# Packed attention with a convolution gate: whole float32 words in batch 0's first layer, and group 4's keys and queries loaded as whole rows

## The chip, the cores and the metric

The kernel runs on one NeuronCore of a Trainium2 chip. It uses five engines with queues of their own: PE (matrix multiplies, with PEld for the loading of the stationary operand), DVE (vector work), ACT (activations and copies), POOL (set-up only here) and SP, which issues the transfers; transfers run on 16 DMA engines. The metric is the device time of one execution in microseconds (us), as a median over runs.

## What is computed

Batch 8, 8 heads, 576 positions, 64 numbers per head; p holds 32 packed queries per head. q, k, v and p come as float32, the three weights as float64.

```python
def sm_attn(qq, kk, vv):
    s = scale * np.matmul(qq, kk.transpose(0, 1, 3, 2))
    s = s - np.max(s, axis=-1, keepdims=True)
    a = np.exp(s)
    a = a / (np.sum(a, axis=-1, keepdims=True) + 1e-09)
    return np.matmul(a, vv)
p_packed = sm_attn(p, k, v)
out = sm_attn(q, p_packed, p_packed)
...
h = np.maximum(x @ w_in, 0.0)           # x: [B, S, 512], w_in: [512, 1024]
conv_out = sum(conv_w[k] * hp[:, k:k + S, :] for k in range(3))
gate = 1.0 / (1.0 + np.exp(-conv_out))
return (h * gate @ w_out).astype(np.float32)
```

So there are two attentions (the packed queries read the sequence, then the sequence reads the 32 packed rows), a first layer with relu, a gate from a convolution over three positions, and a second layer.

## The kernel before

**Tiling.** Four heads make a group; a batch has two groups, so there are 16 groups (group g belongs to batch g // 2). A group's attention (`attention`, L489) runs: first scores on PE (L450), their maximum on DVE (L495), exp on ACT (L499), the transposed weights (on PE at L525 with a copy at L528, from group 10 on by DVE and 16 transfers), the product with the values (L535), scaling and a transpose (L546, L551, L554), second scores (L450), then the second softmax on DVE and ACT (L559 to L578) and a transpose back (L583). The softmax's result is kept as two fp32r parts: `a2hi` (ACT, L587) and the remainder `a2lo` (DVE, L589).

The packed rows are multiplied with `w_in` beforehand: `packed_weight(b, hf)` (L599) gives, for each half hf of the 1024 columns, a weight `gw` for the batch, again as two parts: `ghi` by a copy on ACT (L621), and `glo`, for batches 0 and 1 by subtracting `ghi` in PSUM with PE (L625) and a second copy on ACT (L629), later with DVE (L632). `ffn1(b, j)` (L640) is the first layer, one of eight blocks of 128 columns: twelve fp32r multiplies of 288 columns (two groups, two halves of the sequence, and the products hi·hi, lo·hi, hi·lo) at L661; relu (L673), the three taps (L677, L679, L683), tanh (L687) and the gate (L689). `ffn2(m)` (L710) is the second layer for 128 rows of the output, with 24 multiplies of 512 columns (L752), a copy (L760) and the store (L762).

**Weights.** Eight tiles: 0 to 3 are parts of `w_in` (the first half of the columns needs 0 and 1, the second 2 and 3), 4 to 7 of `w_out`. Each is loaded (`load_weight`, 1024 KB) and made from float64 into float32 by ACT (L265) and DVE (L267, L272); those of `w_out` are split further by ACT, PE (L328) and ACT.

**Keys and queries** come in two ways (`by_block`, L356). For groups 0 to 3 a tensor is one transfer of whole rows (576 KB, 128 pieces of 4608 B), transposed on PE in nine 128 x 128 transposes, five and then four (L434), each set copied by ACT (L440). From group 4 on it is four transfers of 144 KB with pieces of 128 B (L405) and one DVE transpose (L417).

**Order.** `ORDER` (L21) is a text of two-digit numbers in base 36, each naming a stream (a load, a group's attention, a step of a layer); at each mention the stream's next step is issued. Every engine and SP works its queue in this order. `Flow` (L64) is a plan of times beside it: it reckons when each step would start, and before the second layer starts it puts multiplies of the identity into PE's queue wherever PE would wait (`fill`, L133; `warm`, L241, L244). Transfer times in the plan are multiplied by the factors in `SLOW` (L84).

**Buffers.** Accumulation tiles `big` in PSUM have three buffers, shared by scores, PE transposes, `packed_weight`, the weight split and the first layer; `h` has three, `gw` two, `a2` four, and `kq` three for the loads of groups 2 and up.

The order before, by queue, at its beginning (T5 and T4 are the two sets of PE transposes, s1 and s2 the scores, pv the product with the values, pk `packed_weight`, f1 b.j `ffn1`):

- SP: k0, q0, p(0), k1, w2, v0, conv_w, k2, w0, q1, v1, w1, k3, p(1), q2, v2, w5, w3, k4, w4, q3, v3, w6, k5, w7, v4, ...
- PE: kT0 T5, kT0 T4, qT0 T5, s1(0), kT1, ..., pk(0,0), pv(2), s1(3), minus(0,0), s2(2), f1 0.0, f1 0.1, f1 0.2, pk(0,1), ...
- DVE, from group 0's second softmax on: L559(0), maximum, w0 first half, subtract, w0 second half, sum, multiply, maximum of group 2, L583(0), w1 first half, L559(1), maximum, subtract, w1 second half, sum, a2lo(0), multiply, L583(1), ..., a2lo(1), ...

Of the kernel before, what the change touches and what calls it, by code (L numbers as in the profile page):

```python
# [18 lines left out]


ORDER = (  # L21
    "0002043m0408043u0304030305060b3l0c06013k050b060c0g0c0c0b060605053q3v3k0e06070e070a3k063v06063k0j060e3v09060j3s0k"
    "0f0j0o060k0e0f3n0k0i0h3r3r060k0d063k0e0m0d3k3r060d0r0e0e0d060e060e060m060e0m0r3t0m0m3t0s0r400e3w0w0s0e0s0n0z0e0e"
    "3t0s0l0e0n060z0z0l0l0e3y170e46460m0q060m0e0u0e0u0l0m460m0e41460p410m170m0e0m0u17480u3x493x480v410v0m0u3x48410m4a"
    "49484a10474849474a3z0m414948413z491f4a49124248470u0u4a4a474b124b0t490u124b0t14433z0u0t0m4a434b0m4c0t4d1f4b4b434c"
    "0u441f4d0x4c4b3z12120u4e18434e3z1a0u4c120m4d4c4g3o6e130u1a154c3z0u131a124c6e450m0u434e4d45126e0u4e434g4f0m456e4g"
    "1a0u1n0m0u124f6e1n451l4d4e4f6e0u454f4d1a4h1c4e4e0u0u4f4g1b0y1k4d451b4i4f4f114j4i7e1n7e4k4i6e1g4h6f4j6e6e4i6f6e4k"
    "4h4k4i4j4i7f161i121a4k4j4i6e1i6f6f121e1a4j4k4l7f1d126f6f6f6f4j4k4l1i6f1o4k6g121s4l1i4l6g4h124l7g4m1a4l6f1a1j4m1q"
    "191j1i1a6f4m4j121i6g1q7g1w6g6h6e4n6g4m6h1q204n1a1v6g1i6g4m1v4l1h6g4m1a4n124m121r1v4n6g6g236f7h1a6g4o121i4n1i4o4p"
    "6h6h4o4p4p1a236h124o7h4o6h4n1q6g4p1a6h6h6h4p6h4o1m4o1a1y4n234p4p1q1i6h1i1q4q282b1y4r6i1r1y6i1y1a1i6i126i6i1q1a2b"  # L30
    "4r6i12241a4q4q1z6i6j1a6i1a4r1i6i6i4s6i2b1p4s6j4s1q4t4u1q4s1i1y1i4t4s264t1t4t1q1z6k1y2g6j2c4u6j1y4u4s261i6j2j4u6j"
    "4s6k6j264u2j4v4t2j1q6j271i4u1u4v226i4u6j266j4t2e1x4w2k6j4t1i4v1q2e1i1q6k4w2e4v2a1i1q6h2f2e4v3p6k6k6k4w1y1i274x26"
    "6k1q6k6l1y4x6l216k6k6k2f4x1q6k4x2m1y4v50266m1q6l6l4w264v1q2r2m6l2h4w6l2m2r506l4x2r6l4y4w1q4y291y6l6l4w501q4y6l6m"
    "4z6m4z262o2n4x1q6m4z2e6m4y6m6m2z1y4x4z6m264y4y4z524z1y4y52524z6l6m251y522s6m34536n535354542e6m2m542e26512u526n6n"
    "6o6n546j6n261y516n532z54526n2z6n6n6n52541y376n516o376p5554553753536m6o262u6o2w552e5630266o6o55266o5635535655266o"
    "6o57552n5756551y56566o2i6p6o1y586p262u6p586q562e596p262d58596p6p6n596p2m6p1y586p6q58576p2m2e6o2u57595a1y5732592m"
    "6q2l1y58586q57266q596q6q3232572m3f2m6q362q6q592e266r6q5b6q262m6r3f2e265a5b6r6r6s6p6r6r5a5c2m6r6s2e5d6r6r5c2e6r5c"
    "5d2m5b5c5c5d5e6r2m6s2e5c6s5e325c5f2u2e5d5e5e6r5d5d383f5e5f2e6s5f5e336s6s6t2v5f6s6s2e6t5k3a2m5d2p2u6s5f5f6s5k5g6t"
    "5e2m3c5g3a2x6t5g2v6t5h2m6t2e6q2m6t2u6t6u2e325k2m6t6u5h2u6t5h6t5f5h5i5h6t3g5h2e5i6u2m5i6u2t2y6u6u5h6u5j333a3a6v5g"
    "6u5j2u6u6u5i5g5i5j326u6v2u3i5j2m5i5j5j5i6v6v6v2m5g5m2u6v6u5m5j5m2u5n6v2u5g325m6v3a6v6w5m6v3d5m3i6w5n5n6v5o5m6w6w"  # L40
    "32313i6w3b6x3i6w5n32325o3a5l5n5o6w3j5l6v5o6w6x32326w6w5o3b325n2u325p6w6x6y5n325l5p3j6x5q6s5o5o6x3a2u5r6x6x5p6x5p"
    "2u5q5q5r6x6x5r6y5p5p3a5q3i6x3e6z5r5p325s2u5q6x325q5s2u5r6y2u6y6y6y3a5q5s5t6z396y2u6y5r5r6y5t6y3a3i5u5t5s6y5t5s3a"
    "325s2u5t325t5s5u325v5t6z326z6z5u6z6w6z3i703i6z703i6z3a6z5v5w5w5v3a5x6z3a5y703a5w5x5w705y5w5w703h5y7070705y5w706y"
    "705x5x713a70715z5z3a5x5y3i64715y703i3i715x3i5x5y5z7172713a5z5z3i3a6071716071603a605z7161717264603i6z60613i723i3a"
    "3i5z726172727271617260727261627372627373626274636261733i73616473743i653i6263736573637363636273736673636674747466"
    "6367676667747474667466687574676872746675676967657568676969767569756a6969756976757575756b6a75776a686a76766a6b6b76"
    "6a7676767675766b76776a6c77786c77776b766b6b7768686c776d6d776c776d7777786c6d6c686d7878786c74786d787878786d79797a79"
    "79797979797a787979787b7a7a7a7a7977797b7a7a7a7a7c7a7b7b7b7b7a7b7b7c7b7b7b7c7c7d7c7c7d7c7c7c7c7d7d7d7d7d7d7d7b7c7d"
    "7d7d7d7d7d7d7i7d7d7c7d7i7d"
)  # L50


# [132 lines left out]
def tile_packed_attention_conv_gate(  # L185
# [303 lines left out]
    def attention(g):  # L489
        G = grp[g]  # L490
        yield Step("PE", 556, after=[("pT", g), ("kT", g)] + [("s1", g - 1)] * (g > 0), take=["big", "a1"], give=["kT", "pT"], sets=[("s1", g)], cols=1152, tiled=True)
        t = score(G["pT"], G["kT"], g)
# [90 lines left out]
        nc.vector.transpose(out=at, in_=s2)  # L583
# [56 lines left out]
    def ffn1(b, j):  # L640
# [15 lines left out]
        for gg in range(NG):
            ah, al = grp[NG * b + gg]["a2"]
            for w, xs in ((hi, (ah, al)), (lo, (ah,))):
                for x in xs:
                    for hf in range(2):  # L660
                        nc.tensor.matmul(  # L661
                            out=t[:, hf, :SH],
                            lhsT=w[:, gg, js],
                            rhs=x[:, hf * SH : (hf + 1) * SH],
                            start=n == 0,
                            stop=n == 3 * NG - 1,
                        )
# [153 lines left out]
```

## Time and profile before

| | us |
|---|---|
| median of 3 runs | 407.02 (406.36 to 407.58) |
| profiled execution | 406.22 |
| its span | 404.4 |
| PE busy | 395.5 (98% of the span) |
| DVE busy | 340.2 (84%) |
| ACT busy | 275.2 (68%) |

A span runs from the first to the last instruction of the profiled execution; the execution's own time is 1.8 us longer. Busy time is the union of an engine's instructions. In the rows below, a line of a group shows the source line, engine and operation, output and inputs with their shapes and count, then busy time and the mean of one in ns, then idle time just before it and what released it. A line of the order of time begins with start and length in us. The page gives the granted PE clock as full in every fortieth of the span, and the DMA engines as nearly full in the first fifth.

### The profile page before, as it was taken

The numbers are of one execution on the slowest core, as the hardware profiler recorded it, in microseconds if no ns is written. First come the engines' busy times: TensorE is split into PE (matmuls) and PEld (weight loads), VectorE is DVE, ScalarE is ACT, GpSimd is POOL, SyncE is SP. The second block draws the span as 40 slices with busy tenths as digits, with TensorE's granted clock in tenths as the row PEclk, the third lists the DMA queues.
The fourth block names the chain that finished last, engine by engine and source line by source line (L and its number), as shares of the span: only waits on it lengthen the run. The fifth ranks groups of instructions, "written<-read, shape, count | busy, mean of one in ns | idle before, by whom it ended". The sixth has DMA issues, their size and how long they took to land.

```text
span 404.4 us, 8231 instructions
## 1 busy us (share of the span) xinstructions
PE 395.5 (98%) x3319; PEld 317.6 (79%) x3319; DVE 340.2 (84%) x494; ACT 275.2 (68%) x475; POOL 0.9 (0%) x12
## 2 busy tenths in 40 slices
PE   7899999999999999999999999999999999999996
PEld 6668677787868878888778788788687878887886
DVE  0789999999999999999999999999889886557220
ACT  4889999977668486867566756687666676655121
POOL 0000000000000000000000000000000000000000
PEclk9999999999999999999999999999999999999999
DMA  8999999997947876496563715316001000010211
GB/s 298 366 366 233 293 257 163 137 157 128 134 96 105 129 190 128 88 186 103 107 99 99 151 55 101 129 30 113 28 2 52 28 18 35 26 53 0 78 53 52
DMA packets 140377, 49.19 MB, mean 122 GB/s; under 512 B 121244, under 2 KB 132788, under 8 KB 140340
## 3 DMA queue, kind: packets, MB, share of 16 engines
q1 hardware_dynamic: 140340, 48.67, 53.9%
q8 instruction: 26, 0.43, 0.5%
q14 instruction: 11, 0.09, 0.1%
HBM read 37.25 MB, written 9.44 MB: 115 GB/s over the span
## 4 chain that ended last, share of the span: by engine, by line
PE 74%; DMA 8%; ACT 8%; DVE 5%; SPq 3%; issue 1%; ACTq 0%
PE fo L752 42%; PE big L661 19%; PE sm L752 3%; DMA hgt<-in_moe_w_in_dram 3%; PE big L450 3%; PE big L609 2%; PE sm L535 2%; SPq L515 2%; DMA s<-in_moe_conv_w_dram 2%; DMA v<-in_v_dram 2%; ACT hgt L677 1%; ACT hbuf L673 1%; ACT hgt L687 1%; ACT wo_hi L323 1%; PE big L525 1%
## 5 line engine op out<-in xcount | busy, mean ns | idle before, releaser
L752 PE MATMUL fo<-wo_hi,xhi 128*128 128x512 f32 (+1 forms) x272 | 109.8, 404 | 0.7 <-ACT o L760 0.7
L752 PE MATMUL fo<-wo_hi,xlo 128*128 128x512 f32 (+1 forms) x272 | 106.5, 392 | 0.0
L752 PE MATMUL fo<-wo_lo,xhi 128*128 128x512 f32 (+1 forms) x272 | 106.1, 390 | 0.0
L673 ACT ACTIVATE hbuf<-big 128x576 f32<-128x576 f32 x64 | 41.8, 657 | 32.2 <-PE big L661 32.1
L752 PEld LDWEIGHTS fo<-wo_hi,xhi 128*128 128x128 f32 x272 | 51.2, 188 | 15.7 <-issue 3.0
L679 DVE SCALAR_TENSOR_TENSOR hgt<-hbuf,cw,hgt 128x576 f32<-128x576 f32 x64 | 51.2, 806 | 13.7 <-ACT hgt L677 13.3
L752 PEld LDWEIGHTS fo<-wo_hi,xlo 128*128 128x128 f32 x272 | 51.1, 188 | 12.3
L703 DVE TENSOR_TENSOR xlo<-hgt,xhi 128x1024 fp32r<-128x1024 f32 (+1 forms) x44 | 44.7, 1021 | 16.7 <-ACT xhi L700 16.6
L752 PEld LDWEIGHTS fo<-wo_lo,xhi 128*128 128x128 f32 x272 | 51.1, 188 | 8.5
L661 PE MATMUL big<-a2hi,ghi 128*128 128x288 f32 x256 | 55.8, 299 | 0.1
L687 ACT ACTIVATE hgt<-hgt 128x576 f32<-128x576 f32 x64 | 43.7, 690 | 15.9 <-DVE hgt L683 15.7
L661 PE MATMUL big<-a2hi,glo 128*128 128x288 f32 x256 | 54.4, 294 | 0.0
L661 PE MATMUL big<-a2lo,ghi 128*128 128x288 f32 x256 | 54.2, 293 | 0.0
L683 DVE SCALAR_TENSOR_TENSOR hgt<-hbuf,cw,hgt 128x576 f32<-128x576 f32 x64 | 50.8, 804 | 0.4
L689 DVE SCALAR_TENSOR_TENSOR hgt<-hgt,hbuf 128x576 f32<-128x576 f32 x64 | 47.2, 744 | 4.6 <-ACT hgt L687 4.3
L677 ACT ACTIVATE hgt<-hbuf,cw 128x576 f32<-128x576 f32 x64 | 49.8, 783 | 0.9
L661 PEld LDWEIGHTS big<-a2hi,ghi 128*128 128x128 f32 x256 | 42.9, 188 | 5.9 <-ACT glo L629 1.0
L700 ACT CAST xhi<-hgt 128x1024 fp32r<-128x1024 f32 (+1 forms) x44 | 38.9, 891 | 10.8 <-PE fo L752 6.4
L760 ACT COPY o<-fo 128x512 f32<-128x512 f32 (+1 forms) x34 | 19.6, 578 | 33.3 <-PE fo L752 28.7
L661 PEld LDWEIGHTS big<-a2lo,ghi 128*128 128x128 f32 x256 | 40.9, 188 | 0.0
L661 PEld LDWEIGHTS big<-a2hi,glo 128*128 128x128 f32 x256 | 40.8, 188 | 0.0
L495 DVE TENSOR_REDUCE nm<-big 128x1 f32<-128x576 f32 x16 | 11.9, 746 | 10.6 <-PE big L450 10.6
(91 smaller groups left out, 494.1 us busy)
## 6 DMA issues: line engine op xcount, KB each, us to landing
out_dram<-o SPq DMA_DIRECT2D x35, 256.0 KB, 2.5
v<-in_v_dram SPq DMA_DIRECT2D x16, 512.0 KB, 5.8
k<-in_k_dram SPq DMA_DIRECT2D x48, 144.0 KB, 4.1
q<-in_q_dram SPq DMA_DIRECT2D x48, 144.0 KB, 4.1
hgt<-in_moe_w_in_dram SPq DMA_DIRECT2D x3, 1024.0 KB, 11.2
hgt<-in_moe_w_out_dram SPq DMA_DIRECT2D x3, 1024.0 KB, 6.5
a1T<-stage SPq DMA_DIRECT2D x96, 20.0 KB, 1.8
hgt<-in_k_dram SPq DMA_DIRECT2D x2, 576.0 KB, 5.0
```

Source lines behind the costliest of these rows:

```text
L450: nc.tensor.matmul(out=o.rearrange("c (j r) -> c j r", r=NR) if by_block(g) else o, lhsT=lhs[r, 32 * i : 32 * i + 32], rhs=rhs[r, :, h, :] ...
L661: nc.tensor.matmul(out=t[:, hf, :SH], lhsT=w[:, gg, js], rhs=x[:, hf * SH : (hf + 1) * SH], start=n == 0, stop=n == 3 * NG - 1,)
L673: nc.scalar.activation(out=h[:, 1 : S + 1].rearrange("c (f s) -> c f s", f=2), in_=t[:, :, :SH], func=AF.Relu, scale=0.5)
L677: nc.scalar.activation(out=d, in_=h[:, 1 : S + 1], func=AF.Copy, scale=cw[:, NJ + j : NJ + j + 1])
L679: nc.vector.scalar_tensor_tensor(out=d, in0=h[:, 0:S], scalar=cw[:, j : j + 1], in1=d, op0=ALU.mult, op1=ALU.add)
L683: nc.vector.scalar_tensor_tensor(out=d, in0=h[:, 2 : S + 2], scalar=cw[:, 2 * NJ + j : 2 * NJ + j + 1], in1=d, op0=ALU.mult, op1=ALU.add)
L687: nc.scalar.activation(out=d, in_=d, func=AF.Tanh)
L689: nc.vector.scalar_tensor_tensor(out=d, in0=d, scalar=1.0, in1=h[:, 1 : S + 1], op0=ALU.add, op1=ALU.mult)
L700: nc.scalar.copy(out=hi[:, js, o], in_=src[:, js])
L703: nc.vector.tensor_tensor(out=lo[:, js, o], in0=src[:, js], in1=hi[:, js, o].bitcast(F32), op=ALU.subtract)
L752: nc.tensor.matmul(out=t[:, : fs.stop - fs.start], lhsT=x[:, c, :], rhs=w[:, c, fs], start=c + i == 0, stop=c == NJ - 1 and i == 2)
L760: nc.scalar.copy(out=o[:, fs], in_=sums_of[m, q][:, : fs.stop - fs.start])
```

## The change

Five things change.

1. `by_block` holds for group 4 too: its keys and queries are one 576 KB transfer each, transposed by PE (18 transposes and four copies on ACT) instead of eight transfers and two DVE transposes. The scores of group 4 read and write their blocks in the other order accordingly.
2. For batch 0 (`WHOLE = 1`) the second softmax's result of groups 0 and 1 stays one float32 tile (`a2whole`, straight from DVE's transpose), and `gw` one float32 tile (one copy on ACT): no `a2hi`, `a2lo`, no subtraction on PE, no second copy.
3. Batch 0's eight first-layer steps multiply whole float32 words: four multiplies of 288 columns in place of twelve in fp32r.
4. The plan's factors for transfer times change, and with them the number and places of the fillers.
5. `ORDER` is new throughout.

```diff
-    SLOW = ((4600, 1.28), (5500, 1.7))
+    SLOW = ((4600, 1.28), (5500, 1.15), (16500, 1.0), (56000, 1.085))
...
+    WHOLE = 1
...
-        return g < NG * 2
+        return g < NG * 2 + 1
...
+        if g < NG * WHOLE:
+            yield Step("DVE", 669, take=["a2"], give=["s2"], sets=[("hi", g), ("a2", g)])
+            at = wk.tile([128, S], F32, name="a2whole", tag="a2hi", bufs=4)
+            nc.vector.transpose(out=at, in_=s2)
+            G["a2"] = (at,)
+            return
...
+        if b < WHOLE:
+            yield Step("ACT", 904, give=["big"], sets=[("gw", b, hf)])
+            whole = wk.tile([128, NG, 512], F32, name="gwhole", tag="ghi")
+            nc.scalar.copy(out=whole, in_=t)
+            gw[b, hf] = (whole,)
+            return
...
-        yield Step("PE", 1563, after=after, take=["big", "h"], give=give, sets=[("f1", b, j)], cols=3456)
-        hi, lo = gw[b, j // 4]
+        whole = b < WHOLE
+        yield Step("PE", 1930 if whole else 1563, after=after, take=["big", "h"], give=give, sets=[("f1", b, j)], cols=4608 if whole else 3456)
+        parts = gw[b, j // 4]
...
+        last = (1 if whole else 3) * NG - 1
         for gg in range(NG):
-            ah, al = grp[NG * b + gg]["a2"]
-            for w, xs in ((hi, (ah, al)), (lo, (ah,))):
-                for x in xs:
+            xs = grp[NG * b + gg]["a2"]
+            for k, w in enumerate(parts):
+                for x in xs[: len(xs) - k]:
                     for hf in range(2):
                         nc.tensor.matmul(
...
-                            stop=n == 3 * NG - 1,
+                            stop=n == last,
```

The new order, by queue, at its beginning:

- SP: p(0), k0, p(1), conv_w, k2, q0, k1, v0, w1, q1, v1, w0, k3, q2, v2, k4, w2, w4, w3, q3, v3, w5, q4, k5, v4, w6, k6, w7, ...
- PE: kT0 T5, kT0 T4, s1(0), qT0 T5, kT1 T5, L525(0), qT0 T4, kT1 T4, pv(0), s1(1), ..., s2(1), ..., qT2 T5, pk(0,0), qT2 T4, pv(2), s1(3), kT4 T5, s2(2), f1 0.0, kT4 T4, f1 0.1, L525(3), f1 0.2, s1(4), qT3 T5, f1 0.3, the split of w4, pk(0,1), pv(3), qT3 T4, f1 0.4, f1 0.5, ...
- ACT, around the first step of the first layer: whole copy of gw(0,0), pb(2), qT2's second copy, ppT(2), queries of group 5, `minus`, kT4's first copy, exp of group 3, two of the queries, w2, relu of f1 0.0, ...
- DVE, from group 0's second softmax on: L559(0), maximum, subtract, w1 second half, sum, maximum of group 2, multiply, w0 first half, L559(1), w0 second half, maximum, subtract, whole transpose (0), sum, multiply, maximum of group 3, whole transpose (1), L559(2), ...

Runs of PE steps that use 64-row or 32-column tiles (s1, s2, pv, pk) without another step between number 29 in the old order and 26 in the new.

More of the change, by code (lines that the diff above doesn't have):

```diff
@@ L21 @@
 ORDER = (
[L22 to L46, printed above, removed]
@@ L47 @@
-    "6a7676767675766b76776a6c77786c77776b766b6b7768686c776d6d776c776d7777786c6d6c686d7878786c74786d787878786d79797a79"
-    "79797979797a787979787b7a7a7a7a7977797b7a7a7a7a7c7a7b7b7b7b7a7b7b7c7b7b7b7c7c7d7c7c7d7c7c7c7c7d7d7d7d7d7d7d7b7c7d"
-    "7d7d7d7d7d7d7i7d7d7c7d7i7d"
+    "3m030300043n3k0g030b0b0404040b020j06060508010c3k0j06060505070c060c3s0j06070a3k0c093k3q0e060o0605063k0e060e3t0k0i"
+    "0k0k3t060f060k0e0e0h3k060f060d3t0r060d0d0m0e0e0d0e0e060e060m060m0m3r0r0w0r0s3r0e0z3r0s0e0e0m0n0s0z0s0l0z060e0l46"
@@ new lines @@
+    "0l0m0n0u3u0e460m0m0l100m0m0e170e173l100e0u0e0u0m3y0m17480v1f3v103v3w4810490m0u483z493v0q4a0u3z480v49480p484a123z"
+    "0t491f3x0t3z484a3x40123x124b3z0y0m494a494b0m471f4b490u474a4a414b0m0t4c410t4a0m3z144d0u4c41120x0u4241414b4b4c1c0u"
+    "0m12440u183o4b4d4c0m416e1a4c1n4c1k134e4d430u6e0u4c4e110m1n6e4e430u110u436e431n134f4d4f1a4g1a0u121g4e4545431a0u0m"
+    "4g454g1b1243120u6e111a1b4d456e154f0u4e4d12110u454g4f4d120u121a4e451i1a1m0u4f4h1v1i4e1v4f4i4f1i4i4j7e1v4i1o4k7e12"
+    "4j6e4i4j121a6f6f4k6e6e6e4h4h7f166e121i1d4j6f4i196f4k1s6f4j1i1q1a4j124k121i1t1e1j4j1j7f234k1a1i4h6f231q6f4i1q4k12"
@@ new lines @@
+    "4i231a6g4l122b6f4m4m4k1a1w6f4l6f1q6g6e1i127g1i4n1l1h4m1q4l1y1a6f1q4m4n1y4l4l4n1i1y1r4q6g6g7g1a4l286g1r6h4n4m126g"
+    "4l4m6g1i4o6g6g1a4o6g201z4n1y244m214p1q4o1u4o4n6h6g7h4p2b1i4o6h6h2b1q4p1z7h1a6h4o6h6g4p1a4p4p6h6h6h6h4n1q4o4p124r"
+    "1y6i6h1a6i4q6h2j1a1y261i4q1a1a4r6i6i6i1p266i6i2c4s1i264s6i4r4s266i4s6f6j264t1i1q4s2e4t4t274s6i6j1i4u1q1y4t1y1i2o"
+    "6i4s6j2e6j4u6k6j1y6j4u2j1q1i4t4u2p1i4t2j4v6j2e6j276j4t4v6j6j1x3p6k4w4v1i6k2g4w502k26221y4w2e4v4w26504u6l1q2m4w4u"
+    "1y294v506k1q6k4w6k6k4u6l2r6k6j4v2w6k4v6k6k4x1y6l6m6l4x1i1q2r4x6l2r6m2z6l6l4y6k2f6l1q2m6i266l1q4w2m1q1y1q2e4y6l4y"
@@ new lines @@
+    "4x4y1y4x251q264y6l2f1q4x4z4x6m4z6m6m4z6m2m4z4y6m2z6m2z522q2s522e4z26374y4z2u512652514z6n532h2n6m535252532a6n266m"
+    "54526m6n536n52536n536l6n516n6n2u542m266o6n55541y6n546m2u53556o2e6n56306p5454556p6o2d2e1y3e546o1y1y6o2e562n566o56"
+    "6o6o6o1y6o576q572u2e6o2v56552e5a322m57565726566p2m26576p5a581y6p26576n552i556p586p6p6p576p26591y586q58262v2m2632"
+    "6p2l6q2u35596q595859326q58266o596q59582m6q556q59266r2e3c6q6q6p6q6r2e2u2e2m325b6r2x6r6r6q6r6r6s5a5c5c5c2e2t2m2e6r"
+    "2m2m5d5c5c6r2u2u5b2e2m6r5c346r2u6s5b5e5e335c335e6t2m6s5e5e6s2m2e6s5d5f372e5e6s5f6s5e6s5f6s5g5d325g6s5f5d386t5d6s"
@@ new lines @@
+    "5k2u373a2e5k5f6u322u6t6t325f2u3a6t6t6t6t3f5g3a3f6s2m6t6t5f2y5d6t6u5h6v6u3a6u5h5g6u2u5g2m2e5g5d6r3f6u5h6u6u6v2m2m"
+    "3b2u6u5i5i5k5g6u2u5j3g5i5h6u6v6v2m3a315i5j322u5h5j2u6v6v5h5l325i5h323a3i5i323b6v5j5j2u5j5m6v6u365i6v5m3i5m5j5n3i"
+    "3d6w5n5m6w6v5o6v5m6w6w6t5n5o6w5m6v6w5o6w6w5n325n5o5m6x5l5n6w6w6w5p6x5n5l5q6w6x5p3i6x2u6y6x5o6x6x5q6x6y3a5p5p5p6x"
+    "5q2u325o5o5p5q5p6x3i6x325r396y5s6y6y5r5q6y325q2u6x5s5q6z325r5t6y5t325r5r3a5s3a6y5t6y5r6y3j5u3i3a325u6y6z325v3j5s"
+    "6z5s6z5t6z5t5r5s325t5s3i325t6z5u6z6z703i5v6z6z6z703i3a5w5x5w5w7071705w703h5x5w70705w5x706y703a5y715x5w5z5y705y5x"
@@ new lines @@
+    "5v3i5y5y705x64713a713i5y717272713a64713a5z713a5z715x71603a70715y3a615z5z3a7272606073606171607260723i727272736160"
+    "723a5z723i625z61733i3i63733i3i733i73726161733a733i6364626363743i737462626373657363743i6162746z627462747466636566"
+    "677474666666677475756865746775767568756768756866686676757575686875696a73756967676a76697674766a69766967776a766975"
+    "69766b6a767676776a6c786b6a77776d6b6c787677776c6d6d776b776d6c776c776d6b777878786c6c6b776b786d6d787879787978787979"
+    "7979787a797979797a7a7a7a7a7a7b797a7a7a7b7b7b7b7b7b7b7c7c7b7b7a797c7d7c7c7b7b7c7c7c7d7c7c7d7d7a7d7c7d7d7d7d7c7d7d"
@@ L50 @@
+    "7i7i7d7d7d7d7d7d7d7d7d"
 )
```

## The prediction

> **What bounds the kernel now.** I read the page's first line, then the busy time by stretches, then the order of time on PE.
>
> ```profile
> span 404.4 us, 8231 instructions
> ```
> ```profile
> 0.00:50.00 50.00, 45.32 (x549) 34.06 (x549) 36.68 (x61) 41.32 (x83) 0.90 (x12) 1.00 0.99 313
> 10.00:20.00 10.00, 8.34 (x117) 6.24 (x117) 7.36 (x15) 9.06 (x21) 0.00 (x0) 1.00 1.06 367
> 30.00:75.00 45.00, 44.47 (x465) 31.96 (x458) 44.28 (x69) 44.19 (x74) 0.00 (x0) 1.00 1.02 229
> 50.00:380.00 330.00, 328.97 (x2658) 265.57 (x2658) 300.32 (x432) 229.52 (x386) 0.00 (x0) 1.00 0.51 98
> ```
> Columns: stretch, its length, busy PE, PEld, DVE, ACT, POOL, then clock, DMA share, GB/s. From 50 to 380 us PE has 1.0 us of gaps in 330. So the end is the moment at which PE has its first uninterrupted supply, plus the PE work then left. What PE wastes lies before 50 us: 4.7 us of gaps, and multiplies of the identity that only fill waits.
>
> ```profile
> L244 PE MATMUL idle<-ident 128*128 128x128 f32 x68 | 11.6, 305 | 1.5 <-POOL ident masks.py:199 1.5
> ```
> ```profile
> 35.00:404.00 369.00, 1.21 (x8) 1.15 (x8) 1.00 0.50 101
> ```
> ```profile
> 33.10 1.73 PE L244 MATMUL idle<-ident 128*128 128x128 f32 x14
> 34.58 0.50 PE L661 MATMUL big<-a2hi,ghi 128*128 128x288 f32 x2
> ...
> 44.72 0.83 PE L244 MATMUL idle<-ident 128*128 128x128 f32 x6
> 45.88 0.90 PE L535 MATMUL sm<-v,a1T 128*32 128x64 f32 x40 [0.32 <-DMA v<-in_v_dram]
> ```
> The fillers take 11.6 us, 1.2 of them after 35 us (second row, of the filler alone). The first large piece, step 0 of the first layer for batch 0 (L661), starts at 34.58, straight behind fillers. Behind it 1.5 us are wasted: those 1.2 and the 0.32 before 45.88, where the values of group 3 are late. So all depends on when that step starts and on what PE work is added.
>
> **Term A: the first step starts earlier.** DVE rows of the way there (start, length):
>
> ```profile
> 15.78 0.78 DVE L559 STREAM_TRANSPOSE s<-big 128x576 f32<-128x576 f32 x1 [0.33 <-PE big L450]
> ...
> 17.93 0.76 DVE L565 TENSOR_TENSOR s<-s,mx 128x576 f32<-128x576 f32 x1
> 18.59 1.23 DVE L272 SCALAR_TENSOR_TENSOR w_in_sb<-hgt 128x1024 int32<-128x1024 int32 x1
> 19.73 0.75 DVE L572 TENSOR_REDUCE sm<-s 128x18 f32<-128x576 f32 x1
> ...
> 23.98 0.69 DVE L267 TENSOR_SCALAR hgt<-hgt 128x1024 int32<-128x1024 uint32 x1 [0.84 <-DMA hgt<-in_moe_w_in_dram]
> 24.79 0.78 DVE L559 STREAM_TRANSPOSE s<-big 128x576 f32<-128x576 f32 x1
> ```
> Start to start a 576-column pass takes 0.66 us (17.93 to 18.59), a transpose some 0.03 more, and the second half of a weight conversion 1.14 (18.59 to 19.73).
>
> Loads come first. Their sizes are 576 KB for keys, queries or values of a group, 1024 KB for a weight tile, 128 for p; they land at the 367 GB/s of 10 to 20 us, when the DMA engines are full (896 KB take 2.5 us). Up to group 1's values the old order issues 6232 KB, the new one 5336: 896 KB or 2.5 us earlier. Both weight tiles of the first half (w0, w1) are complete at 7256 KB before and 6360 after, again 2.5 us, and the 0.84 us stop at 23.98 goes. Against it, group 1's keys move behind k2 and q0 (1856 KB to 2584: 2.0 us later), and their PE transposes stand ahead of group 0's; k0 moves behind p0 (0.4 us). Group 0's values come 0.8 us sooner. I take the first L559 as unmoved: 15.7.
>
> From there the new DVE order has, up to group 1's L559: L559 0.71, maximum 0.67, subtract 0.66, conversion of w1 1.14, sum 0.67, reciprocal and small ones 0.45, group 2's maximum 0.67, multiply 0.67, first half of w0 0.61, and about 0.5 of waiting for ACT's exp: 6.8, so 22.5 in place of 24.79. After it: L559 0.71, w0 1.14, maximum and subtract 1.33, whole-word transpose of group 0 0.70, sum and reciprocal 1.07, multiply 0.67, group 3's maximum 0.67, transpose of group 1 0.70, with 0.4 of waiting 7.4: 29.9. Now no a2hi on ACT and no a2lo on DVE (L589, below) follow. What is late next is PSUM: `big` has three buffers, and on ACT the copy of group 4's transposed keys and group 3's exp (0.7 each) free them, at 30.1 and 30.9. One wait is new on PE: group 4's transposed keys need k4, issued with 8664 KB, so about 3.9 us behind the w1 that came at 23.98: 27.9. PE gets there at about 28.5; behind it in PE's queue stand group 2's second scores and the first-layer step itself, which wants nothing before 29.9, so that k4 may be 2 us late at little cost. I take the start as 30.7 instead of 34.58: **A = -3.9**; bounds 29.9 and 32.5 (ACT a full weight conversion late): -4.7 to -2.1.
>
> **Term B: PE work added behind that start.** Steps ahead of it are the same on PE, except one subtraction pass (L625) out and five transposes in, which cancel.
>
> ```profile
> 84.36 1.59 PE big L661 x12
> ```
> ```profile
> 56.47 1.02 PE L328 MATMUL big<-tmp,ident 128*128 128x512 f32 x2
> ...
> 57.56 1.02 PE L328 MATMUL big<-tmp,ident 128*128 128x512 f32 x2
> ```
> ```profile
> 25.63 1.17 PE L434 MATMUL big<-ident,k 128*128 128x128 f32 x9
> 26.64 0.61 PE L244 MATMUL idle<-ident 128*128 128x128 f32 x4
> ```
> ```profile
> 92.05 0.40 PE L752 MATMUL fo<-wo_hi,xlo 128*128 128x512 f32 x1
> 92.37 0.72 PE L450 MATMUL big<-kT,pT 64*32 64x288 f32 x16
> ...
> 94.33 0.50 PE L752 MATMUL fo<-wo_hi,xhi 128*128 128x512 f32 x1
> 94.67 0.40 PE L752 MATMUL fo<-wo_lo,xhi 128*128 128x512 f32 x1
> 94.91 0.39 PE L752 MATMUL fo<-wo_hi,xlo 128*128 128x512 f32 x1
> ```
> A step of the first layer is now 12 fp32r multiplies, 1.59 us. Whole float32 multiplies with 128 rows and 288 columns do not occur in the first layer; the nearest is L328: 1.09 us from one pair to the next, of which the fp32r one of 512 columns is 0.24 (94.67 to 94.91), so 0.85 for 512 whole columns, 1.66 ns a column. A new step has 4 x 288 columns: 1.92, with the gaps between records 1.95. So +0.36 x 8 = +2.9 (bounds: 1.90 by columns alone, +2.5; 2.2 if each of eight weight loads shows 0.03 more, +4.9). Thirteen transposes at (26.64 - 25.63) / 9 = 0.112 are +1.45; the second subtraction pass goes, -0.6. **B = +3.75.** All of it is on the path, since PE is full there.
>
> The Trainium skill speaks against these transposes: TensorE: Matmul & The Clock Gate, Part 4: PE-mode transpose, gives about 275 ns for one in a kernel. At that estimate the thirteen would cost 3.6 us and not 1.45, and the sum below would be +0.7. The row at 25.63 speaks for 112 ns back to back, so I give that estimate no chance of its own.
>
> **Term C: gaps behind the start.** Group 3's values have 13912 KB issued up to them before, 12888 after, and no keys in 144 KB pieces among them:
>
> ```profile
> 61.42 3.92 SPq L405 DMA_DIRECT2D k<-in_k_dram  x4
> ```
> Issuing four pieces holds SP 3.9 us, where little else is in flight; one 576 KB load lands in 1.6 at the rate above. So the values are some 5 us earlier (2.8 by bytes, 2.3 by pieces) and the stop at 45.88 goes. Were the pieces hidden all the same, 2.8 would do. What is late next is ACT (44.19 of 45 us busy in 30 to 75), which must drain the steps' PSUM. It loses two a2hi and two second weight copies and gains four copies of transposed keys and queries:
>
> ```profile
> L587 ACT CAST a2hi<-a2t 128x576 fp32r<-128x576 f32 x16 | 11.0, 686 | 1.7 <-DVE a2t L583 1.7
> L629 ACT CAST glo<-big 128x1024 fp32r<-128x1024 f32 x4 | 4.1, 1035 | 0.0
> L440 ACT COPY kT<-big 128x640 f32<-128x640 f32 x4 | 2.8, 698 | 4.3 <-PE big L434 4.3
> L417 DVE STREAM_TRANSPOSE kT<-k 128x1152 f32<-128x1152 f32 x12 | 16.4, 1366 | 0.2 <-PE big L450 0.2
> L589 DVE TENSOR_TENSOR a2lo<-a2t,a2hi 128x576 fp32r<-128x576 f32 x16 | 11.8, 737 | 0.3 <-ACT a2hi L587 0.2
> ```
> That is 3.4 off and 2.6 on for ACT; DVE loses two L417 and two L589, 4.2. Stepping through the new order from 30.7, I find PE short pauses of 0.2 to 0.45 us before steps 3 and 4, the w4 pass and step 5, together 1.0: **C = -0.5** (bounds -1.5, no pause; +1.5, pauses twice the old ones).
>
> **Term D: fewer changes between small and full multiplies.** Entering a run of 64-row multiplies costs 0.09 more than the step before (0.32 against 0.23), leaving it 0.10 in the next (0.34 against 0.24), and some drain. The new order has 26 such runs, the old 29: between 0.6 and 1.1 us, **D = -0.7**. The freed DVE time later and the changed transfer order of groups 5 to 15 I cost at nothing: PE covers them, with 1.0 us of gaps in 330; were that cover gone, they could lose as much again.
>
> **Sum**: -3.9 + 3.75 - 0.5 - 0.7 = -1.4 us. The profiled execution took 406.2 (span 404.4), so 404.8; the median of the runs is 407.02, 0.8 above it, and moved by the same amount is **405.6**.
>
> **Rivals.**
> 1. *ACT and DVE free PE fully.* For it: both are the full engines from 30 to 75 us and have less to do. Start at 30.2, no pauses: -4.4 + 3.75 - 1.5 - 0.7 = -2.9, 404.1. Against it: ACT's gain is 0.8 only. Chance 0.20.
> 2. *PSUM starves PE: slower.* With whole words batch 0 needs fewer passes, but the copies of group 4 (0.6 to 0.7 each) go into a full ACT queue ahead of the exp and relu that free `big`; PE has nothing else that needs no `big`. If each of six refills is 0.4 late, the start is 31.9 and the pauses 3.0: -2.7 + 3.75 + 1.5 - 0.7 = +1.9, 408.9. It decides from about 1.5 us of lost ACT time before 50 us. Chance 0.16.
> 3. *The gain is eaten*: the work added equals the time saved, with the pauses as before and D hidden: -3.9 + 3.75 = about 0, 406.9. Chance 0.14.
> 4. *The PE clock falls back.*
> ```profile
> 4.58 2.18 PE L434 MATMUL big<-ident,hgt 128*128 128x128 f32 x9 [0.56 <-DMA hgt<-in_k_dram]
> ```
> At 4.58 us nine transposes took 2.18 us, twice as long as the nine at 25.63, after PE had done little. If the new early order, with more of them, let this happen again for 3 us of work, it would cost 1.5: 407.1. Nothing after 7 us shows it, the granted clock is 1.00 throughout. Chance 0.03. The same section of the Trainium skill states that transposes do not count as PE activity for the clock gate; no stretch here is long enough to test it.
>
> **How the numbers follow.** The forecast has 0.47. Differences under 0.3% (1.2 us) can't be told from no change; -1.4 lies just beyond, so about 0.29 of the forecast's chance is faster and 0.18 within. Faster: 0.29 + 0.20 = 0.49. Within: 0.18 + 0.14 + 0.03 = 0.35. Slower: 0.16. The range goes from rival 1's time less half a microsecond, 403.6, to 408.0, which leaves out most of rival 2.
>
> **What would show it.** L661 of batch 0 with `a2whole` starting near 30.7; its steps 1.95 us apart when back to back; L434 with 90 transposes near 0.11; SP without the four 144 KB pieces before group 5; fillers under 9 us in total; no stop before group 3's L535. I am wrong if the first step starts after 32, if a step takes over 2.1, or if PE shows more than 2 us of gaps and fillers between 31 and 75, or more than 2 after that.

## The result and the profile after

| | median, us | range, us | runs | ratio to the kernel before | 95% |
|---|---|---|---|---|---|
| before, in the same measurement | 406.31 | 405.93 to 407.58 | 10 | | |
| after | 408.36 | 406.86 to 411.05 | 10 | 1.0057 | 1.0039 to 1.0075 |

The change makes the kernel slower by about 2 us where a gain of 1.4 was forecast, and its runs spread over 4.2 us where those before spread over 1.6. The profiled execution of after took 408.1 us. The first rows are from its page (span, busy time by engine, and the group of the new first-layer multiplies):

```profile
span 405.9 us, 8121 instructions
...
PE 396.1 (98%) x3267; PEld 314.2 (77%) x3267; DVE 337.1 (83%) x490; ACT 274.1 (68%) x475; POOL 0.9 (0%) x12
```
```profile
L676 PE MATMUL big<-a2whole,gwhole 128*128 128x288 f32 x64 | 17.2, 412 | 0.1
```
PE is as full as before (98%), with 0.6 us more work and 0.9 us more idle time. 64 records for eight steps show that each whole-word multiply is recorded twice.

**The start.** The order of time on PE, then SyncE's queue (SPq: start, and how long issuing held it), then two rows of DVE, then two more of PE, all of after:

```profile
6.49 1.33 PE L435 MATMUL big<-ident,hgt 128*128 128x128 f32 x5 [1.78 <-DMA hgt<-in_k_dram]
...
10.09 1.21 PE L451 MATMUL big<-kT,pT 64*32 64x288 f32 x16
...
12.50 0.71 PE L435 MATMUL big<-ident,hgt 128*128 128x128 f32 x5
```
```profile
0.74 0.44 SPq L468 DMA_DIRECT2D p<-in_p_dram  x1
1.24 0.49 SPq L395 DMA_DIRECT2D hgt<-in_k_dram  x1
```
```profile
18.11 0.78 DVE L560 STREAM_TRANSPOSE s<-big 128x576 f32<-128x576 f32 x1 [0.21 <-PE big L451]
...
24.69 0.78 DVE L560 STREAM_TRANSPOSE s<-big 128x576 f32<-128x576 f32 x1
```
```profile
32.49 2.21 PE L676 MATMUL big<-a2whole,gwhole 128*128 128x288 f32 x8
...
47.96 4.32 PE L676 MATMUL big<-a2whole,gwhole 128*128 128x288 f32 x16
```
The keys of group 0 are issued second, at 1.24, and land at 6.44 (4.53 before); PE waits 1.78 us for them. What follows on PE runs at about half pace: five transposes take 1.33 us at 6.49 and 0.71 at 12.50. So the first transpose back on DVE comes at 18.11 where it came at 15.78 before, and the first first-layer step at 32.49: 2.09 us earlier than before, not 3.9. The granted clock is shown as full here (1.00 from 0 to 13 us). The Trainium skill (TensorE: Matmul & The Clock Gate, table "Why this matters for your kernels") asks for about 4 us of busy PE before matmuls reach full pace and says that idle gaps over about 3 us undo it. The rows agree with the first half, in that the slow work lies in the first 12 us; they do not show that the gap makes it slow. It was shorter than the one that the page names, and w7_early, an experiment below, waits only 0.27 us at this place and is as slow.

**A stall much later.** SyncE's queue, ACT and PE in after:

```profile
192.26 10.68 SPq L516 DMA_DIRECT2D a1T<-stage  x16
202.99 0.58 SPq L379 DMA_DIRECT2D v<-in_v_dram  x1
203.62 0.66 SPq L383 DMA_DIRECT2D v<-in_v_dram  x1
204.38 0.55 SPq L777 DMA_DIRECT2D out_dram<-o  x1
```
```profile
208.55 0.59 ACT L775 COPY o<-fo 128x512 f32<-128x512 f32 x1 [2.70 <-DMA out_dram<-o]
```
```profile
209.19 0.50 PE L767 MATMUL fo<-wo_hi,xhi 128*128 128x512 f32 x1 [1.31 <-ACT o L775]
```
Read from the bottom: PE stands 1.31 us until ACT has copied an output tile out of PSUM, and ACT until an earlier tile's store has left its buffer. That store was issued at 204.38, behind sixteen small `a1T` transfers, whose issue alone held SyncE for 10.68 us. The kernel before has no such wait until its tail (0.68 us at 367, which after has too).

**The ledger.** For this table each multiply on PE is counted from its start to the start of the next, though no longer than its own record; the rest is a gap. All in us; (n) is a number of records. The third kernel is an experiment that comes below.

| | before | after | difference | stores_pool |
|---|---|---|---|---|
| first first-layer step starts at | 34.58 | 32.49 | -2.09 | 30.57 |
| from there on: first layer | 102.69 | 105.38 | +2.69 | 105.40 |
| transposes of keys and queries | 1.16 (9) | 2.54 (22) | +1.38 | 2.60 |
| second pass for `glo` | 1.59 | 1.02 | -0.57 | 1.02 |
| 64-row and 32-column runs | 38.97 | 38.74 | -0.23 | 38.72 |
| second layer | 205.81 | 206.04 | +0.23 | 206.08 |
| other | 13.85 | 13.68 | -0.17 | 13.66 |
| fillers | 1.18 | 0.33 | -0.85 | 0.22 |
| gaps | 1.35 | 2.44 | +1.09 | 1.14 |
| last multiply ends at | 401.19 | 402.65 | +1.46 | 399.39 |

From the first step on, the added work is 3.50 us (first layer, transposes, second pass). The start gave 2.09 back and the waiting nothing. That is the loss of 1.46 at the last multiply; the profiled executions differ by 1.9, and the other 0.4 comes behind the last multiply, 0.3 of it outside the span, where the ledger doesn't reach.

### The profile page after: what moved, and what is told of

It is laid out like the page before. It is cut to its first block, busy times and chain, and to the rows that moved or that the text cites. A ratio compares the mean times of both kernels' runs of the same rounds, so it can differ in the third digit from the quotient of the medians.

```text
span 405.9 us, 8121 instructions
## 1 busy us (share of the span) xinstructions
PE 396.1 (98%) x3267; PEld 314.2 (77%) x3267; DVE 337.1 (83%) x490; ACT 274.1 (68%) x475; POOL 0.9 (0%) x12
## 4 chain that ended last, share of the span: by engine, by line
PE 82%; ACT 13%; DMA 2%; DVE 1%; issue 1%; SPq 0%; ACTq 0%
PE fo L767 45%; PE big L676 22%; PE sm L767 3%; PE big L451 3%; PE big L616 3%; PE sm L536 2%; ACT hgt L692 2%; ACT hgt L702 1%; DMA hgt<-in_k_dram 1%; ACT hgt L266 1%; PE big L435 1%; ACT hbuf L688 1%; DMA out_dram<-o 1%; ACT a L500 1%; ACT wo_hi L324 1%; ACT wo_lo L333 1%
## 5 line engine op out<-in xcount | busy, mean ns | idle before, releaser
L676 PE MATMUL big<-a2hi,ghi 128*128 128x288 f32 x224 | 48.2, 296 | 0.0
L676 PE MATMUL big<-a2hi,glo 128*128 128x288 f32 x224 | 47.5, 293 | 0.0
L676 PE MATMUL big<-a2lo,ghi 128*128 128x288 f32 x224 | 47.4, 293 | 0.0
L676 PEld LDWEIGHTS big<-a2hi,ghi 128*128 128x128 f32 x224 | 38.0, 188 | 5.0 <-DVE s L560 0.8
L676 PEld LDWEIGHTS big<-a2lo,ghi 128*128 128x128 f32 x224 | 35.8, 188 | 0.0
L676 PEld LDWEIGHTS big<-a2hi,glo 128*128 128x128 f32 x224 | 35.7, 188 | 0.0
```

The lines of the kernel that those rows point to most:

```text
L676: nc.tensor.matmul(out=t[:, hf, :SH], lhsT=w[:, gg, js], rhs=x[:, hf * SH : (hf + 1) * SH], start=n == 0, stop=n == last,)
```

## The experiments

Each kernel was timed against the kernel before on the same chip.

| kernel | median, us | range, us | runs | ratio | 95% |
|---|---|---|---|---|---|
| k0_first | 407.37 | 405.42 to 409.78 | 12 | 1.0019 | 1.0000 to 1.0038 |
| warm_start | 409.10 | 407.21 to 412.77 | 11 | 1.0060 | 1.0035 to 1.0085 |
| out10_early | 408.01 | 406.52 to 409.14 | 12 | 1.0034 | 1.0019 to 1.0050 |
| whole_off | 413.97 | 412.89 to 415.79 | 5 | 1.0174 | 1.0148 to 1.0200 |
| rows_off | 413.41 | 412.93 to 414.10 | 4 | 1.0170 | 1.0152 to 1.0189 |
| before_whole | 407.54 | 407.40 to 408.12 | 12 | 1.0028 | 1.0016 to 1.0040 |
| before_rows | 411.20 | 410.43 to 411.38 | 5 | 1.0113 | 1.0097 to 1.0128 |
| w7_early | 409.38 | 408.47 to 409.90 | 6 | 1.0069 | 1.0054 to 1.0084 |
| two_moves | 406.90 | 405.74 to 410.90 | 12 | 1.0023 | 1.0001 to 1.0045 |
| moves_lo | 407.11 | 405.22 to 410.54 | 12 | 1.0016 | 0.9994 to 1.0037 |
| both_old | 410.29 | 410.01 to 410.44 | 4 | 1.0099 | 1.0083 to 1.0115 |
| stores_pool | 405.33 | 404.61 to 407.58 | 12 | 0.9981 | 0.9965 to 0.9997 |
| after_pool | 406.66 | 405.21 to 408.74 | 12 | 0.9999 | 0.9982 to 1.0017 |
| before_pool | 407.42 | 407.13 to 408.84, and one of 1071.97, left out of the ratio | 12 | 1.0030 | 1.0018 to 1.0042 |

**The start: k0_first and warm_start.** In the first, group 0's keys go ahead of the first block of p; in the second, PE gets eight fillers ahead of the first transposes of those keys, which stay where they are.

```diff
-SP: p(0), k0, p(1), conv_w, k2, ...
+SP: k0, p(0), p(1), conv_w, k2, ...
```


> The changed kernel with one transfer moved: group 0's keys are issued ahead of the first p tile, as before the change. Theory 1 (the late keys and the PE clock that rises late cost about 1.8 us of the expected early start): keys land near 4.6 instead of 6.4 us, the first first-layer step starts 1.0 to 2.0 us earlier than 32.5, and the whole is 1.0 to 2.0 us faster than the changed kernel (ratio to before 1.001 to 1.003). Theory 2 (PE work added and late stalls explain the loss): the start may move, the time stays within 0.5 us of the changed kernel's 408.4.

```diff
+            if g == 0 and name == "k" and lo == 0:
+                warm(8)
             t = big().rearrange("r f s -> r (f s)")
```


> The changed kernel with eight more multiplies of the identity on PE just ahead of group 0's first transposes, where PE now waits 1.8 us for the keys; transfers as in the changed kernel. If the late rise of the PE clock by itself is what costs (steps at half pace until 12 us), full pace comes near 8 us, the first first-layer step moves 0.7 to 1.5 us earlier and the time falls by as much. If only the late keys cost, the start stays at 32.5 +- 0.3 and the time at the changed kernel's.

The order of time on PE and on DVE in k0_first, on PE in warm_start, and the first five transposes in w7_early and in moves_lo (both described below; the first issues its beginning as after does, the second as k0_first does):

```profile
5.42 0.71 PE L435 MATMUL big<-ident,hgt 128*128 128x128 f32 x5
...
7.59 0.72 PE L451 MATMUL big<-kT,pT 64*32 64x288 f32 x16
```
```profile
15.82 0.78 DVE L560 STREAM_TRANSPOSE s<-big 128x576 f32<-128x576 f32 x1 [0.21 <-PE big L451]
...
22.40 0.77 DVE L560 STREAM_TRANSPOSE s<-big 128x576 f32<-128x576 f32 x1
```
```profile
3.73 4.34 PE L245 MATMUL idle<-ident 128*128 128x128 f32 x20
7.91 0.71 PE L437 MATMUL big<-ident,hgt 128*128 128x128 f32 x5
...
9.89 0.72 PE L453 MATMUL big<-kT,pT 64*32 64x288 f32 x16
```
```profile
4.98 1.33 PE L435 MATMUL big<-ident,hgt 128*128 128x128 f32 x5 [0.27 <-DMA hgt<-in_k_dram]
```
```profile
5.75 1.27 PE L435 MATMUL big<-ident,hgt 128*128 128x128 f32 x5
```
With the keys first, the first-layer step starts at 30.80, 1.69 us sooner than in after, and the ratio falls from 1.0057 to 1.0019. One profile is one execution, though. In four kernels that issue their first 32 us alike (after, out10_early, after_pool, w7_early) the first step starts at 31.57 to 32.60; in four with the keys first (k0_first, two_moves, moves_lo, stores_pool) at 30.57 to 31.30. By the means of these eight the move is worth 1.1 us at this point, and the medians of after and k0_first differ by 1.0. What it does change in every profile is the landing of the keys: 4.28 to 4.52 in the four with the keys first, 4.93 to 6.44 in the seven of the new order that have p ahead.

In warm_start PE has its full pace (0.71 for five transposes), but the fillers last until 7.9, past the landing of the keys, and the first scores come at 9.89 where after has them at 10.09; the first step, at 31.91, lies within the range above. So pace alone, bought with fillers, buys nothing; the keys have to come sooner. When PE reaches full pace differs between executions (five transposes take 0.71 in k0_first and 1.27 in moves_lo, behind the same 14 fillers), and no run here shows what decides it.

**The store stall: out10_early and two_moves.** Two stores move ahead of what held SyncE; two_moves does this and has the keys first.

```diff
-SP: ..., a1T(12) x16, v, store 10, k15 x4, store 11, ...
+SP: ..., store 10, a1T(12) x16, v, store 11, k15 x4, ...
```


> The changed kernel with two stores moved in SP's queue: tile 10's store ahead of group 12's sixteen moves, tile 11's ahead of group 15's keys. Theory: the 1.3 us stop of PE at 209 us, where the second layer's copy waits for an output buffer that a store still holds, goes, and the time falls by 0.8 to 1.3 us. Rival: PE meets the next wait at once (the moves of group 12 are late by as much), 0 to 0.3 us.

> The kernel after with both moves that were tried singly: the first group's keys issued ahead of the first position block, and the stores of output tiles 10 and 11 moved ahead of the long key and query issues. Theory 1 (the late start and the store stall are two separate costs): the gains add. k0_first was 1.0 us below the kernel after, out10_early 0.35 us, so 406.7 to 407.4 here, with the first first-layer step near 30.8 and under 0.8 us of PE waiting for ACT's copies of the outputs near 209. Theory 2 (what is saved in one place is waited for in another, since PE has the same work left): no better than k0_first alone, 407.4 to 408.2.

What PE waited for in two_moves, over the whole span (us in total, times, longest):

```profile
PE sm L536 <- DMA a1T<-stage: 0.9, 3, 0.3
PE fo L767 <- ACT o L775: 0.7, 1, 0.7
```
The stall at 209 us is gone (the 0.7 left lies in the tail, as in the kernel before). In its place PE waits 0.9 us, between 228 and 231 us, for the next sixteen `a1T` transfers: their issue begins at 217.52, where k0_first begins it at 215.60. In out10_early the same wait is 0.8. The medians are 0.35 us below after (out10_early) and 0.5 below k0_first (two_moves), both within the intervals. So moving a store in that queue trades one wait for another, which suggests that the queue, not the place in it, is short; stores_pool below tests this.

**The spread: w7_early.** In after the load of weight tile 7 is issued behind the four small-piece loads of group 6's keys, which it passes here.

```diff
-SP: ..., w6, k6 x4, w7, p, ...
+SP: ..., w6, w7, k6 x4, p, ...
```


> The changed kernel with one load moved: weight tile 7 ahead of group 6's keys (four 144 KB loads of 128 B pieces that held SP's queue 7.7 us). Theory 3 (tile 7 lands at 64.5, less than 1 us before DVE wants it, and in some executions after that; this makes both the loss and the wide scatter): tile 7 lands before 60, the runs lie closer together (a spread under 2.5 us where the changed kernel had 4.2) and the median falls by 0.5 to 1.5 us. Rival: the scatter comes from the start or the stores, and spread and median stay.

SyncE's queue and DVE in after; then DVE and PE in warm_start; then SyncE's queue and DVE in w7_early:

```profile
50.89 7.74 SPq L406 DMA_DIRECT2D k<-in_k_dram  x4
58.67 0.68 SPq L296 DMA_DIRECT2D hgt<-in_moe_w_out_dram  x1
```
```profile
65.34 0.69 DVE L268 TENSOR_SCALAR hgt<-hgt 128x1024 int32<-128x1024 uint32 x1
```
```profile
66.33 0.70 DVE L268 TENSOR_SCALAR hgt<-hgt 128x1024 int32<-128x1024 uint32 x1 [1.45 <-DMA hgt<-in_moe_w_out_dram]
```
```profile
68.46 0.73 PE L640 MATMUL big<-ghi,minus 128*128 128x512 f32 x2 [1.47 <-ACT ghi L636]
```
```profile
50.27 11.49 SPq L406 DMA_DIRECT2D k<-in_k_dram  x4
```
```profile
64.32 1.38 DVE L418 STREAM_TRANSPOSE kT<-k 128x1152 f32<-128x1152 f32 x1 [1.63 <-DMA k<-in_k_dram]
```
In after the tile landed at 64.51 and was used at 65.34, so it had 0.8 us to spare; before, it landed at 56.83 and was used at 63.82, 7.0 to spare. In warm_start's profiled execution it missed: DVE stood 1.45 us and, behind it, PE 1.47; in after_pool's it missed by 0.6. With the tile ahead, the six runs lie within 1.4 us of each other, the fastest at 408.47; the median is a microsecond higher than after's, though the intervals of the ratios overlap. In the profiled execution the keys of group 6 are late in place of the tile, as DVE's 1.63 shows. So one late transfer took the place of another there. That w7 makes up the spread is supported by six runs only, and not shown.

**The parts alone: whole_off, rows_off, before_whole, before_rows, both_old.** The first two undo one part in the new order; the next two put one part into the old order; the last puts both into it.

```diff
 whole_off
-    WHOLE = 1
+    WHOLE = 0
 rows_off (before_rows and both_old the other way round)
-        return g < NG * 2 + 1
+        return g < NG * 2
```
Steps that a part drops or adds go out of the order, or right behind the step that they need.

> The changed kernel with batch 0's first layer back in two fp32r parts (twelve multiplies a step), the dropped copies and subtractions put back right behind their first halves; transfers and all else in the new order. If whole words pay (an earlier start worth more than 0.45 us x 8 of PE work): slower than the changed kernel by 0.5 to 2.5 us, with the first step near 35. If whole words are themselves the loss: faster by 1 to 2 us.

> The changed kernel with group 4's keys and queries again in four loads of 128 B pieces and one DVE transpose each; the place in the order is that of the new loads and of the first PE set. If whole rows pay: slower by 1 to 6 us, because the pieces hold SP's queue ahead of three weight tiles and group 3's values, and the first step waits for more of DVE. If they are the loss (2.0 us of PE work): faster by 0.5 to 2 us.

> The kernel before with whole float32 words for batch 0 and nothing else: order and plan factors as before, the dropped steps left out. PE work +0.45 x 8 - 1.2 = +2.4 us; the first step at about 31.5 instead of 34.6 because it no longer waits for the second parts. If the earlier start comes back in full: -1.5 to 0 us against before; if the later waits (third weight tile, group 3's values) eat it: +1 to +2.5.

> The kernel before with group 4's keys and queries as whole rows and PE transposes, and nothing else: order and plan factors as before. PE work +2.0 us; off the path 2.7 us of DVE and the 12.6 us for which the pieces of group 4's keys hold SP. If PE work counts in full: +1.0 to +2.5 us against before. If the freed engines give it back: -1.0 to +0.5.

> Both parts of the change (whole rows for group 4, whole words for batch 0) in the order of the kernel before, with the steps that are gone taken out of it and the added copies put right behind their transposes. Theory 1 (each part adds PE work and the new order is what makes room for it): the two single losses add, 406.3 + 1.2 + 4.9 = 412.4, range 411.5 to 413.4, so that the new order is worth about 4 us. Theory 2 (the two share a cause: before_rows loses at one place where PE waits for the copies of the transposed queries, which ACT reaches sooner once it has no parts to make): 408.5 to 411.

PE in rows_off, and PE in before_rows:

```profile
32.08 5.75 PE L245 MATMUL idle<-ident 128*128 128x128 f32 x50
```
```profile
77.20 0.66 PE L434 MATMUL big<-ident,q 128*128 128x128 f32 x4 [0.78 <-ACT qT L440]
...
78.53 0.53 PE L661 MATMUL big<-a2hi,ghi 128*128 128x288 f32 x2 [0.68 <-ACT qT L440]
```
In the new order, either part undone moves the first step back: to 36.53 without whole words, to 37.67 without whole rows, where PE runs 50 fillers ahead of it. So in an order that was made for both, each part is needed for the early start; how much of this is the part and how much the misplaced order, these two runs don't separate. In the old order, whole words start the first step at 33.02, 1.56 earlier, and cost 2.83 us of PE time behind it: 1.2 us slower, with the narrowest range (0.72) of the kernels with ten or more runs. Whole rows start it 0.67 later (less than starts differ between executions of one order) and cost 4.26 behind it, of which 2.58 are transposes' work (27 records where before has 9, 1.16) and the waits shown: nothing in the old order stands between the two sets of transposes while ACT copies. Both together came out at 410.29, not at the 412.4 of the sum: the two do not add, and the new order is worth 1.9 us (410.29 to 408.36), not 4. whole_off lost 5.6 us against after and before_rows 4.9 against before, each more than either of its expectations allowed.

**PE's work alone: moves_lo.** On top of two_moves, the low parts of batch 1's weights are made by DVE.

```diff
-    PE_LO = 2
+    PE_LO = 1
```


> two_moves, and the low parts of batch 1's packed weights made by DVE (as batches 2 to 7 do already) where PE's second pass and ACT's copy made them: PE loses its last four second-pass matmuls, 1.0 us, ACT two copies of 1.02 us; DVE gets two subtractions of 1.21 us. Theory 1 (PE's work sets the time from the first first-layer step on): 0.5 to 1.1 us below two_moves. Theory 2 (DVE and ACT are as full as PE between 35 and 75 us, so DVE's 2.4 us come out on the path): 0.5 to 2.5 us above two_moves.

By the ledger PE loses the 1.02 us of the second pass and gains 1.15 us of gaps (2.17 to 3.32) behind the start; the median does not move by an amount that can be told. Both expectations missed. The rows of busy time between 35 and 75 us (length, then PE, PEld, DVE, ACT, POOL, clock, DMA share, GB/s), in after and in moves_lo, and then PE's longest wait of moves_lo in that stretch (total, times, longest):

```profile
35.00:75.00 40.00, 39.55 (x383) 24.88 (x381) 39.59 (x61) 39.80 (x67) 0.00 (x0) 1.00 0.98 228
```
```profile
35.00:75.00 40.00, 38.48 (x377) 23.81 (x376) 39.78 (x61) 38.16 (x64) 0.00 (x0) 1.00 1.03 212
```
```profile
PE sm L536 <- DMA v<-in_v_dram: 0.9, 1, 0.9
```
In after PE, DVE and ACT are in balance there. In moves_lo PE and ACT have time left and DVE alone is full, but most of what PE lost went into one wait for a group's values, which took 6.7 us from issue to landing where they took 4.8 in two_moves. So this run shows PE's saved work gone into waits; it does not decide which engine bounds this stretch.

**SyncE's queue: stores_pool, after_pool, before_pool.** Output tiles 0 to 27 are stored through GpSimd's queue: on top of k0_first, on after, and on the kernel before.

```diff
-        nc.sync.dma_start(out=out.rearrange("b s f -> (b s) f")[m * 128 : (m + 1) * 128, fs], in_=o[:, fs])
+        queue = nc.gpsimd if m < 28 else nc.sync
+        queue.dma_start(out=out.rearrange("b s f -> (b s) f")[m * 128 : (m + 1) * 128, fs], in_=o[:, fs])
```


> k0_first (the kernel after, the first group's keys issued ahead of the first position block) with the stores of output tiles 0 to 27 issued by GpSimd's queue, which issues nothing in the kernel after, and not by SyncE's; their places in the order stay. Theory 1 (what is left of the loss is SyncE's queue: the stores stand behind some 11 us of sixteen small a1T transfers, and moved ahead of them, as in two_moves, they make those late): neither PE's wait for ACT's output copies near 209 (1.3 to 1.6 us in after and k0_first) nor its waits for a1T (0.9 in two_moves) remain; 0.5 to 1.6 us below k0_first's 407.4, so 405.8 to 406.9, level with the kernel before. Theory 2 (the transfers themselves are what is short, or GpSimd issues a store much more slowly): no gain over two_moves, 406.9 or more, with PE waits for transfers left in the records.

> The kernel after as it is, with the stores of output tiles 0 to 27 issued by GpSimd's queue; the first group's keys stay behind the first position block. Theory 1 (two separate parts of the loss, SyncE's queue and the late keys): 1.0 us above stores_pool, 405.9 to 406.9, so that SyncE's queue was worth 1.5 to 2.5 us of the kernel after. Theory 2 (the store stall is only the 1.3 us seen near 209, and is partly waited for elsewhere): 407.2 to 408.0.

> The kernel before with the stores of output tiles 0 to 27 issued by GpSimd's queue. Theory 1 (SyncE's queue holds PE only in the new order; the records of the kernel before show 0.3 us of PE waiting for a1T and no wait for output copies but the last): 405.7 to 406.6, no difference that can be measured. Theory 2 (SyncE's queue is short in both orders, and the change costs its PE work whatever the queue): 404.0 to 405.2, below after_pool by as much as before is below after.

Busy time between 200 and 225 us (the same columns) in after, then in stores_pool; then the median time from issue to landing of the stores in stores_pool, and the group of them on POOL:

```profile
200.00:225.00 25.00, 23.69 (x187) 19.44 (x187) 23.25 (x36) 16.45 (x28) 0.00 (x0) 1.00 0.69 140
```
```profile
200.00:225.00 25.00, 25.00 (x198) 20.88 (x197) 24.82 (x38) 15.72 (x28) 0.54 (x1) 1.00 0.66 120
```
```profile
out_dram<-o POOLq DMA_DIRECT2D x28, 256.0 KB, 2.8
...
out_dram<-o SPq DMA_DIRECT2D x7, 256.0 KB, 2.0
```
```profile
L778 POOL DMA_DIRECT2D out_dram<-o x28 | 15.2, 544 | 330.5 <-ACT o L775 309.4
```
With the stores out of SyncE's queue, in stores_pool's profile, PE has no gap between 200 and 225 us (23.69 becomes 25.00), and no wait for `a1T` comes in its place. after_pool is level with the kernel before: 0.9999 against after's 1.0057. stores_pool is 1.1 us faster than the kernel before, the only kernel of the study that beats both. The same edit makes the kernel before slower by 1.0 us, against the expectation of no difference. So the gain is no general one: of the two orders, only the new one gains from relief of this queue. Not all of it is PE's stall, though. From after to after_pool the median falls by 1.7 us and from k0_first to stores_pool by 2.0, but 0.4 and 0.3 of these lie outside the span (time less span falls from 2.17 and 2.13 to 1.78 and 1.80); moves_lo has 1.84 there with its stores left on SyncE, so what sets this part is open. Within the span the gains are 1.25 and 1.7, near the stalls of 1.31 and 1.58. Where the old order loses its 1.0 us was followed only as far as one wait in the records that before doesn't have:

```profile
154.66 0.54 PE L661 MATMUL big<-a2hi,ghi 128*128 128x288 f32 x2 [0.74 <-DVE s L559]
```
A store takes 2.8 us from issue to landing on GpSimd's queue and 2.0 on SyncE's (medians), but the seven on SyncE's are the last ones, with little else in flight. Tiles 0 to 27 take 2.3 in after from SyncE, and 3.2 in the kernel before. The Trainium skill (DMA: Bandwidth & Descriptors, "Latency and other measured facts") gives a first byte after about 1 us for GpSimd's queue and 0.6 for SyncE's; the 2.8 against after's 2.3 agrees with that sign, the kernel before's 3.2 does not, so these runs do not isolate what the queue adds. The last tiles stayed on SyncE because the end of the kernel waits for them.

## Why the prediction was wrong

The forecast was 405.6 us, faster; it came out at 408.4, slower, 0.4 above the range's end. The forecast stood on a median of three runs, 407.02; ten runs gave 406.31 for the kernel before, so the miss in the change itself is larger, +2.05 where -1.4 was expected. By its own terms, with the profiled executions:

- **Term A, -3.9, came out at -2.09.** The step that failed is "I take the first L559 as unmoved: 15.7". The prediction counted group 0's keys behind p as 0.4 us of bytes and left it out of the chain. They landed 1.9 us later in the profiled execution (6.44 against 4.53), and the first transpose came at 18.11. The rest of the chain held: from there 6.58 us to the next (6.8 reckoned) and 7.80 to the first step (8.2). In k0_first the three instants are 15.82, 22.40 and 30.80; the prediction had 15.7, 22.5 and 30.7. In this pair of profiles the step alone is 1.8 us. Executions differ, though: over the four profiles with after's beginning the first transpose comes at 17.21 to 18.11 and the term is -2.0 to -3.0; over the four with the keys first the transpose comes at 15.82 to 16.80. So about 1.1 us is what the keys' place costs, and the near hit of k0_first is partly luck. Even the 15.7 was one execution's: before_pool, with the old order, has 17.23. Rival 4 had a part of the mechanism, transposes at half pace early on, but gave it 0.03; the kernel before has it too (1.33 us for its first five).
- **Term B, +3.75, came out at +3.50.** First layer +2.69 (2.9), thirteen transposes +1.38 (1.45), second pass -0.57 (-0.6). The estimate of 3.6 us from the 275 ns a transpose of the Trainium skill (TensorE: Matmul & The Clock Gate, Part 4: PE-mode transpose) does not hold for transposes in a run: the thirteen cost 1.38. Two whole-word steps back to back are 2.11 us apart in after, where 1.95 was reckoned: eight records 0.24 apart are 1.94, and the first of a step costs 0.1 more. The ledger's 2.69 is still less than eight times 0.52, because batch 0's old steps were also dearer than 1.59: its records take 13.29 us before, 1.66 a step, and 16.19 after, 2.02 a step, which is +2.90 as reckoned. The other batches' first layer takes 0.21 less.
- **Term C, -0.5, came out at +0.24** (fillers -0.85, gaps +1.09). Its pauses in the first 75 us were about as reckoned; the stall of 1.31 at 209 us is what turned the sign. In stores_pool, without it, the term is -1.17.
- **Term D, -0.7, came out at nothing**: -0.23 in the small-tile runs, +0.23 in the second layer. The count of runs, 26 against 29, did not carry over to the time: this term failed whole.
- **"The changed transfer order of groups 5 to 15 I cost at nothing: PE covers them."** This is the second failed step. PE's full queue covered no late store: the store held an output buffer, the buffer held PSUM, and PSUM held PE for 1.31 us. The 1.0 us named for a lost cover was near the size (1.31 in after, 1.58 in k0_first); it should have stood in the sum, or as a rival, since the new order put a store behind a 10.7 us issue. after_pool shows that the queue makes the difference between a loss of 0.57% and none.
- **The rivals.** The slower one (PSUM starves PE early, 408.9) came nearest in time, though by another road: PSUM did hold PE, but 170 us later and through a store. Its own signs, pauses of 3.0 us before 75, did not show.

Taken together, by medians: the keys' place is worth 1.0 us (after to k0_first) and 1.3 (after_pool to stores_pool), the stores in SyncE's queue 1.7 and 2.0. With both mended, in stores_pool, the end moves by 399.39 - 401.19 = -1.8 us where the sum had -1.4, and its median is 1.1 us below the kernel before. The forecast's balance of an earlier start (-4.0 there) against added PE work was sound; the order by which the change was carried out gave the difference away in two places. That the rest of the sum fits as well is luck: in stores_pool Term C is 0.7 better than forecast and Term D, -0.7, is missing.

What stays open: the spread of 2.6 to 5.6 us that the kernels with both parts in the new order keep, w7_early apart, stores_pool too (2.97 us). Late weight and key loads and the 0.7 to 1.0 us by which the start differs between executions are likely causes, not shown ones. Open, too, are the 1.0 us that before_pool loses and the time outside the span.
